# A retention and MLP kernel on one core: a small early read of w1, a last tile in pieces of 384 and 128 columns, and a written-out order of all tasks

## The chip, the cores and the metric

The kernel runs on one core of one Trainium2 chip. The time is device microseconds from one execution of the program; the median of 13 runs of the kernel before is 217.83 us, from 217.11 to 220.94. Engines are named as the profile names them: PE multiplies matrices, DVE and ACT do elementwise work, POOL issues the loads and does a little elementwise work, SP issues stores and transposing transfers.

## The reference

Two stages are chained. The first is a linear attention with a decaying state, over 4 batches, 8 heads, 768 positions and a head width of 64. The second normalises each row of 512, multiplies by a gain, and adds a two-layer MLP with a hidden width of 2048.

```python
gamma = 1.0 - 2.0 ** (-5.0 - np.arange(H))
for t in range(S):
    state = gamma[None, :, None, None] * state + np.einsum('bhd,bhe->bhde', k[:, :, t], v[:, :, t])
    y[:, :, t] = scale * np.einsum('bhd,bhde->bhe', q[:, :, t], state)
# x: y with the heads side by side, (4, 768, 512)
xn = (x - mean(x)) / np.sqrt(var(x) + 1e-06) * g_ln
out = x + np.maximum(xn @ w_ch1, 0.0) @ w_ch2
```

Inputs and output are float32; the kernel multiplies in bfloat16.

## The kernel before

The 3072 rows are cut into 24 tiles of 128 positions. The first position block of each of the four batches comes first (tiles 0 to 3), then the other five blocks of each batch in turn. The recurrence is done block by block: inside a block as a masked product, between blocks through a state per batch.

**A tile's attention.** k and q are transposed so that the head width lies on the partitions. For tiles 0 to 7 PE does it (tasks `e_tk` and `e_tq`, L433 to L446); from tile 8 on SP issues a transposing transfer of k and q together (`e_tr`, L458). DVE scales the transposed q (`e_eq`), PE multiplies (`e_pa`, L472), DVE multiplies by the decay mask (`e_am`), and PE multiplies by v and adds the part from the state (`e_py`, L495). The state comes from POOL scaling v (`e_vg`, L537), PE (`e_pd`, L547) and DVE (`e_pb`). DVE takes mean and variance (`e_bn`) and writes the centred row times the gain (`e_xn`, L514); ACT keeps a copy of x (`e_xc`). The centred rows are transposed by PE and copied by ACT for tiles 0 to 7 (`e_tx`, `e_ex`), and by a transposing transfer on SP from tile 8 on (L593). Because ReLU commutes with a positive factor, the division by the standard deviation is left to the end (`e_sq` on ACT, `e_rs` on DVE).

**The MLP.** Tiles form groups of 1 (eight of them), 2 (four) and 4 (two). A task `e_m1` (L622) is 16 matmuls of 128 columns for a group of one, 8 of 256 for a group of two, or 4 of 512 for a group of four; each needs one quarter of w1, and a ReLU (`e_re`, on ACT or DVE) empties its PSUM tile, of which there are two. The second layer (`e_m2`, L660) is four tasks of four matmuls per tile. Its first task waits for all four quarters of w2. DVE then multiplies by the reciprocal deviation and adds x (`e_add`, L672), and SP stores the tile (`e_st`, L678). The last tile is done in two halves of 256 columns, of which ACT stores the second.

**The loads.** POOL issues all loads of q, k, v, w1 and w2 (L371 and L381), which convert to bfloat16 on the way, except for k and q of tile 0, which SP and ACT load. The constants (two iotas, two memsets of the state) are POOL tasks too. From tile 8 on a one-element copy on POOL, which waits for the load three places earlier, stands before each load of q, k and v (`gate`, L386).

**What sets the order.** Nothing runs as it is written: every piece of work is a task, added to a planner (`Plan.add`) with an engine, a duration, a rank and the tasks that it follows. `Plan.order` (L52) repeatedly takes the task that can start first by its own clock, ties going to the lower rank; pads such as `w_pad`, `tr_pad`, `x_pad` and `slack` lengthen planned waits, and `sq_at` keeps the square roots late. The resulting list is written out, so each engine executes its tasks in that order, and waits in place for whatever a task needs. `Plan.fill` (L113) puts matmuls on zeros before PE tasks whose planned start lies in the first 14 us and leaves a gap.

Of the kernel before, what the change touches and what calls it, by code (L numbers as in the profile page):

```python
# [9 lines left out]
FP32 = mybir.dt.float32  # L10
# [4 lines left out]
PE, ACT, DVE, POOL, SP = range(5)  # L15
# [4 lines left out]
              "k3", "q3", "v3", "w1_2", "k4", "q4", "v4", "k5", "q5", "v5", "w1_3", "w2_0",  # L20
              "k6", "q6", "v6", "k7", "q7", "v7", "w2_1", "w2_2", "w2_3"],
    "bufs": {"qsb": 6, "ksb": 5, "vsb": 9, "qk": 8, "tr": 6, "vg": 3, "trq": 3, "trk": 3},
    "load_pad": 600, "w_pad": 1500, "lead": 32, "lead2": 32, "sq_at": 28000, "late_load": 1250, "step": 8, "pace": 8, "ahead": 3,
    "slack": 600, "tr_pad": 4000, "x_pad": 3000, "vg_pad": 1000, "fill": 0.8, "fill_end": 14000,
}


class Plan:
# [20 lines left out]
        self.tasks.append(t)  # L49
        return t  # L50

    def order(self):  # L52
        left, ends = {}, {}
        for t in self.tasks:
            for u in t["uses"]:
                left[u] = left.get(u, 0) + 1
        held = {name: [] for name in self.bufs}
        engines = sorted(self.seen)
        free = dict(self.begin)
        todo = {e: [t for t in self.tasks if e in t["on"]] for e in engines}  # L60
        sw_free, hw_free, out = self.first_load, 0, []
        while any(todo.values()):
            best = None
            for e in engines:
                for t in todo[e]:
                    if any("end" not in d for d in t["after"] + t["follows"]):
                        continue
                    at = max(free[e], t["at"], sw_free - 7000 if t["load"] else 0)
                    for d in t["after"]:
                        if d["eng"] == e and not d["load"] and not d["hw"]:  # L70
                            at = max(at, d["end"])
                        else:
                            at = max(at, d["seen"] + t["slack"])
                    if t["takes"]:
                        name = t["takes"][0]
                        if len(held[name]) == self.bufs[name]:
                            oldest = held[name][0]
                            if left[oldest]:
                                continue
                            at = max(at, ends[oldest])  # L80
                    if best is None or (at, t["rank"]) < best[0]:
                        best = (at, t["rank"]), t, e
            if best is None:
                raise RuntimeError("no task can start")
            (at, _), t, e = best
            for x in t["on"]:
                todo[x].remove(t)
            t["eng"], t["start"], t["ns"] = e, at, t["on"][e]
            t["end"] = free[e] = at + t["ns"]
            t["seen"] = t["end"] + self.seen[e] + t["lat"]  # L90
            if t["load"]:
                sw_free = max(t["end"] + 800, sw_free) + t["load"]
                t["seen"] = sw_free + 700 + t["lat"]
            if t["hw"]:
                begun = max(at + 600, hw_free)
                queued = max(0, sw_free - begun)
                hw_free = begun + t["hw"] + min(queued, 2 * t["hw"])
                if queued:
                    sw_free += t["hw"] * 2 // 3
                t["end"] = free[e] = max(t["end"], hw_free - 900)  # L100
                t["seen"] = hw_free + 1050 + t["lat"]
            if t["takes"]:
                name = t["takes"][0]
                if len(held[name]) == self.bufs[name]:
                    held[name].pop(0)
                held[name].append(t["takes"])
            for u in t["uses"]:
                left[u] -= 1
                ends[u] = max(ends.get(u, 0), t["seen"])
            out.append(t)  # L110
        return out
# [16 lines left out]
def kernel(  # L128
# [16 lines left out]
    nc = tc.nc  # L145

    B, H, S, D = q.shape
    DM = H * D
    DH = 4 * DM
    P = 128  # L150
    C = S // P
    NT = B * C
    KO = DM // P
# [3 lines left out]
    number = {bc: t for t, bc in enumerate(TILES)}  # L157
# [6 lines left out]
    FILL, FILL_END = CFG["fill"], CFG["fill_end"]  # L164
# [20 lines left out]
    const = ctx.enter_context(tc.tile_pool(name="const", bufs=1))  # L185
# [10 lines left out]
    held = {}  # L196
# [31 lines left out]
    gb = const.tile([P, DM], FP32, name="gb")  # L228
    bns = const.tile([P, NT, 6], FP32, name="bns")
    mv = const.tile([P, NT, 2], FP32, name="mv")  # L230
    rstd = const.tile([P, NT], FP32, name="rstd")
    w1 = const.tile([P, KO, DH], BF16, name="w1")
    w2 = const.tile([P, HO, DM], BF16, name="w2")
# [55 lines left out]
    a = plan.add  # L289
# [109 lines left out]
        load(x, j, pool_rank.get(f"{x}_{j}" if x[0] == "w" else f"{x}{j}", 20 * i))  # L399
    for t, x in ((iota, "iota"), (ipos, "pos")):  # L400
        t["rank"] = pool_rank[x]

    unit, u, behind = {}, 0, []
    for g in range(NG):
# [12 lines left out]
    for t in range(NT):  # L417
        g, i = group_of[t]
# [230 lines left out]

    loaded_w2 = [loaded["w2", i] for i in range(4)]  # L650
    for t, cols in [(t, slice(0, DM)) for t in range(NT - 1)] + [
            (NT - 1, slice(i * DM // 2, (i + 1) * DM // 2)) for i in range(2)]:
        g, i4 = group_of[t]
        hb, h0 = buf_of[g]
        key = ("tp", ("2", t, cols.start))
# [36 lines left out]
                                 rhs=zeros[:, 0:w], start=True, stop=True)  # L692

    with tc.manual_schedule():
        for t in plan.fill(plan.order(), PE, 1100, FILL_END, FILL, warm):
            t["emit"](t["eng"])


# [28 lines left out]
```

## Time and profile before

| | |
|---|---|
| median of 13 runs | 217.83 us (217.11 to 220.94) |
| the profiled execution's own time | 218.1 us |
| its span, first to last instruction | 216.0 us |
| PE busy | 205.3 us (95%) |
| POOL, DVE, ACT busy | 97.2, 118.4, 83.7 us |
| first-layer matmuls (L626) | 93.4 us, 896 of them |
| second-layer matmuls (L664) | 86.9 us |
| matmuls on zeros (L691) | 6.8 us |
| loads through POOL's queue | 13.37 MB, 82% of the time of 16 DMA engines |

The profile is of one execution. A line of it gives the source line (L626), the engine, the operation and the tiles that are written and read. The page cuts the span into 40 slices and gives each engine's busy share in tenths; a busy PE can be matmuls that overlap, so the distance from one start to the next is the better price. The chain of waits follows the work that ended last back to the start. A load's landing is when its data is there, which is later than its issue on the engine.

### The profile page before, as it was taken

To read this page: it belongs to the slowest core of one execution; us is meant where nothing else is said; L and a number is where in the kernel's file an instruction comes from. 1 tells how busy PE (TensorE), PEld (TensorE's weight loads), DVE (VectorE), ACT (ScalarE), POOL (GpSimd) and SP (SyncE) were. 2 spreads that over 40 slices of the span, in tenths; PEclk is the share of its full clock that TensorE was granted. 3 is DMA by queue.
4 is the path that set the end of the run, shared out by engine and by line. 5 is a ranking of instruction groups with operands and counts; after the bars stand their busy time and mean duration, and the time that the engine had idled before them with its cause. 6 is when DMAs were issued, how large, how long until landed. Compare 5 with 4: busy or idle time off the path is not lost.

```text
span 216.0 us, 4747 instructions
## 1 busy us (share of the span) xinstructions
PE 205.3 (95%) x1942; PEld 133.2 (62%) x1962; DVE 118.4 (55%) x230; ACT 83.7 (39%) x157; POOL 97.2 (45%) x151
## 2 busy tenths in 40 slices
PE   7958898999999999999999999999999999999993
PEld 3437798998855458678577667654454444444453
DVE  6847577993157875666786737866553411011121
ACT  5436586665421116345235225305544214442000
POOL 8979569726968666677874746000000000000000
PEclk9999999999999999999999999999999999999999
DMA  9999999999999999999999999921202120010212
GB/s 129 163 180 181 168 191 171 208 108 126 124 168 173 207 154 147 188 159 164 152 148 175 144 164 173 182 72 28 73 0 73 27 97 27 22 49 3 97 49 97
DMA packets 108359, 26.78 MB, mean 124 GB/s; under 512 B 101041, under 2 KB 105393, under 8 KB 108338
## 3 DMA queue, kind: packets, MB, share of 16 engines
q0 software_dynamic: 77024, 13.37, 82.0%
q1 hardware_dynamic: 30114, 12.72, 27.2%
q10 hardware_dynamic: 1200, 0.39, 0.7%
q8 instruction: 15, 0.25, 0.4%
q14 instruction: 6, 0.05, 0.1%
HBM read 27.27 MB, written 6.29 MB: 155 GB/s over the span
## 4 chain that ended last, share of the span: by engine, by line
PE 82%; DMA 8%; POOL 6%; issue 1%; DVE 0%; POOLq 0%
PE tp L664 38%; PE mm L626 34%; DMA w<-in_moe_w_ch_dram 8%; PE pa L477 3%; PE pd L551 2%; PE py L505 2%; PE py L501 2%; POOL qsb L374 1%; POOL vg L539 1%; POOL v L374 1%; POOL ksb L374 1%; POOL vsb L374 1%; POOL w L382 1%; POOL state L287 0%; PE tp L579 0%
## 5 line engine op out<-in xcount | busy, mean ns | idle before, releaser
L626 PE MATMUL mm<-xnt,w 128*128 128x128 bf16 (+2 forms) x896 | 93.4, 257 | 1.0 <-ACT xnt L203 1.0
L664 PE MATMUL tp<-w,h 128*128 128x512 bf16 (+1 forms) x381 | 86.9, 370 | 1.1 <-issue 0.2
L639 ACT ACTIVATE h<-mm 128x512 bf16<-128x512 f32 x91 | 54.4, 598 | 66.4 <-PE mm L626 65.9
L626 PEld LDWEIGHTS <-w 128*128 128x128 bf16 x896 | 66.2, 98 | 21.3 <-issue 1.0
L664 PEld LDWEIGHTS <-h 128*128 128x128 bf16 x400 | 37.7, 98 | 37.5
L673 DVE SCALAR_TENSOR_TENSOR osb<-tp,rstd,x_all 128x512 f32<-128x512 f32 (+1 forms) x25 | 18.2, 729 | 51.3 <-PE tp L664 49.5
L488 DVE TENSOR_TENSOR asb<-pa,mask 128x1024 bf16<-128x1024 f32 x24 | 29.3, 1222 | 12.8 <-PE pa L477 12.8
L520 DVE BATCH_NORM_STATS2 bns<-py 128x6 f32<-128x512 f32 x24 | 16.7, 695 | 19.7 <-PE py L505 19.6
L526 ACT CAST x_all<-py 128x512 bf16<-128x512 f32 x24 | 14.0, 583 | 28.6 <-DVE xn L515 27.5
L539 POOL TENSOR_TENSOR vg<-vsb,vsc 128x512 bf16<-128x512 bf16 x16 | 16.7, 1045 | 8.8 <-DMA vsb<-in_v_dram 6.4
L374 POOL DMA_DIRECT2D vsb<-in_v_dram x20 | 18.2, 911 | 1.7 <-issue 1.7
L515 DVE SCALAR_TENSOR_TENSOR xn<-py,mv,gb 128x512 bf16<-128x512 f32 x24 | 18.0, 751 | 0.9
L565 DVE TENSOR_TENSOR state<-pd,gch 64x256 bf16<-64x256 f32 x40 | 16.7, 418 | 1.6 <-PE pd L551 1.3
L374 POOL DMA_DIRECT2D qk<-in_q_dram x16 | 14.0, 877 | 2.8 <-issue 2.6
L374 POOL DMA_DIRECT2D qk<-in_k_dram x16 | 14.1, 884 | 1.3 <-issue 1.0
L387 POOL COPY scrap<-qk 1x1 bf16<-1x1 bf16 x30 | 5.7, 192 | 13.3 <-DMA qk<-in_k_dram 7.7
L466 DVE TENSOR_TENSOR trq<-tr,qsc 128x512 bf16<-128x512 bf16 x16 | 7.2, 451 | 3.2 <-DMA tr<-qk 3.1
L382 POOL DMA_DIRECT2D w<-in_moe_w_ch_dram x8 | 6.2, 771 | 4.7 <-DMA w<-in_moe_w_ch_dram 4.7
L601 ACT ACTIVATE rstd<-mv,epsb 128x1 f32<-128x1 f32 (+2 forms) x14 | 3.8, 289 | 10.9 <-DVE mv L521 10.9
L691 PE MATMUL pd<-zeros 128*128 128x512 bf16 (+1 forms) x23 | 6.8, 434 | 1.2 <-DVE zeros L237 1.2
L505 PE MATMUL py<-vsb,asb 128*128 128x64 bf16 x160 | 7.9, 193 | 0.0
L501 PEld LDWEIGHTS <-trq 128*128 128x128 bf16 x80 | 6.0, 98 | 3.1
(64 smaller groups left out, 123.2 us busy)
## 6 DMA issues: line engine op xcount, KB each, us to landing
out_dram<-osb SPq DMA_DIRECT2D x23, 256.0 KB, 2.1
w<-in_moe_w_ch_dram POOLq DMA_DIRECT2D x8, 512.0 KB, 9.7
vsb<-in_v_dram POOLq DMA_DIRECT2D x20, 128.0 KB, 5.2
qk<-in_k_dram POOLq DMA_DIRECT2D x16, 128.0 KB, 4.5
qk<-in_q_dram POOLq DMA_DIRECT2D x16, 128.0 KB, 5.0
qsb<-in_q_dram POOLq DMA_DIRECT2D x7, 128.0 KB, 8.5
v<-in_v_dram POOLq DMA_DIRECT2D x4, 128.0 KB, 7.7
ksb<-in_k_dram POOLq DMA_DIRECT2D x4, 128.0 KB, 9.1
```

The lines of the kernel that those rows point to most:

```text
L374: nc.gpsimd.dma_start(out=tile_of(kind, j), in_=src)
L488: nc.vector.tensor_tensor(out=take("asb", t, [P, NPAIR, 2, P], BF16).rearrange("p i a t -> p a i t"), in0=held["pa", t], in1=mask.rearrang ...
L505: nc.tensor.matmul(py[:, h, :], lhsT=held["asb", t][:, h // 2, h % 2, :], rhs=tile_of("v", t)[:, h, :], start=(mi == 0), stop=(mi == n - 1))
L515: nc.vector.scalar_tensor_tensor(out=take("xn", t, [P, DM], BF16), in0=held["py", t].rearrange("p h d -> p (h d)"), scalar=mv[:, t, 0:1], ...
L520: nc.vector.bn_stats(out=bns[:, t, :], in_=held["py", t].rearrange("p h d -> p (h d)"))
L526: nc.scalar.copy(out=x_all[:, t, :].rearrange("p (h d) -> p h d", d=D), in_=held["py", t])
L539: e.tensor_tensor(out=take("vg", j, [P, H, D], BF16), in0=tile_of("v", j), in1=vsc[:, cc, :].unsqueeze(2).to_broadcast([P, H, D]), op=ALU. ...
L565: nc.vector.tensor_tensor(out=held["pb", n][o, :, o], in0=held["pd", b][o, :, o], in1=gch[o, cc, :].unsqueeze(2).to_broadcast([D, NPAIR, D ...
L626: nc.tensor.matmul(p[:, j, :], lhsT=w1[:, ko, (ho + j) * P:(ho + j + 1) * P], rhs=held["xnt", hb][:, h0:h0 + n, ko, :], start=(ko == 0), s ...
L639: nc.scalar.activation(out=dst, in_=src, func=AF.Relu)
L664: nc.tensor.matmul(held[key], lhsT=held["h1", hb][:, ho, i * P:(i + 1) * P], rhs=w2[:, ho, cols], start=(ho == 0), stop=(ho == HO - 1))
L673: nc.vector.scalar_tensor_tensor(out=take("osb", key, [P, w], FP32), in0=held[key], scalar=rstd[:, t:t + 1], in1=x_all[:, t, cols], op0=AL ...
```

## The change

Three things change.

1. A task on SP reads columns 0 to 15 of every row of w1 into a tile `touch` that nothing uses. Its rank is -140.
2. The last tile's output is cut at column 384 instead of 256; SP stores the first piece, ACT the second.
3. `Plan.order` no longer searches. It takes a list `ORDER` of task numbers, in which a number is a task's place among those added (10000 and up also chooses among the engines that may run it), and executes the tasks in that order. The planned times serve only `Plan.fill`. Ranks, `slack` and `sq_at` are no longer read; `w_pad`, `tr_pad` and `x_pad` get smaller.

```diff
-    "load_pad": 600, "w_pad": 1500, "lead": 32, "lead2": 32, "sq_at": 28000, "late_load": 1250, "step": 8, "pace": 8, "ahead": 3,
-    "slack": 600, "tr_pad": 4000, "x_pad": 3000, "vg_pad": 1000, "fill": 0.8, "fill_end": 14000,
+    "load_pad": 600, "w_pad": 550, "lead": 32, "lead2": 32, "sq_at": 28000, "late_load": 1250, "tail": (0, 384, 512), "step": 8, "pace": 8, "ahead": 3,
+    "slack": 600, "tr_pad": 3000, "x_pad": 2000, "vg_pad": 1000, "fill": 0.8, "fill_end": 14000,
 }
+ORDER = [int(x) for x in """
+15 18 14 23 3 8 19 2 27 24 13 26 22 25 44 16 17 45 0 4 7 6 5 28 146 20 21 9 147 10 149 1
...
+314 306 307 690 700 315 298 145 679 327 80 316 311 83 81 540 308 541 538 710 82 84 539
...
+816 817
+""".split()]
...
-    def order(self):
+    def order(self, seq):
...
+        for number in seq:
+            t = self.tasks[number % 10000]
+            e = sorted(t["on"])[number // 10000 % 10]
+            at = max(free[e], sw_free - 7000 if t["load"] else 0)
+            for d in t["after"]:
+                own = d["eng"] == e and not d["load"] and not d["hw"]
+                at = max(at, d["end"] if own else d["seen"])
...
+    touch = const.tile([P, KO, 16], FP32, name="touch")
...
+    a(SP, 390, -140, lambda eng: nc.sync.dma_start(out=touch, in_=w1_v[:, :, 0:16]), hw=400)
...
-            (NT - 1, slice(i * DM // 2, (i + 1) * DM // 2)) for i in range(2)]:
+            (NT - 1, slice(i, j)) for i, j in zip(CFG["tail"], CFG["tail"][1:])]:
...
-        for t in plan.fill(plan.order(), PE, 1100, FILL_END, FILL, warm):
+        for t in plan.fill(plan.order(ORDER), PE, 1100, FILL_END, FILL, warm):
```

Counting the tasks as they are added gives the new order of each engine. POOL's first tasks were iota, iota, v0, k1, q1, v1, the first quarter of w1, k2, q2, the second quarter, v2; they become k1, iota, iota, q2, q1, the memsets of the state, k2, v0, v1, the first and the second quarter of w1, v2. After the fourth quarter of w1 came the first of w2, six tile loads and the other three quarters; now come eight tile loads, one quarter, v8, and the other three, so that k, q and v of tile 8 lie ahead of the last of w2. PE's first tasks were the transposes and product of tile 0, the gain's broadcast and tile 1's transposes; they become nearly the same with k of tile 1 earlier. The first second-layer task was tile 0's, after the first-layer tasks of tiles 0 to 5; it becomes tile 2's, after those of tiles 0 to 5 and two of tile 6. The task numbered 145 is the read into `touch`.

## The prediction

> **What bounds the kernel now.** I read the page first, then busy time by stretch, the chain of waits, and the timeline at both ends.
>
> ```profile
> span 216.0 us, 4747 instructions
> PE 205.3 (95%) x1942; PEld 133.2 (62%) x1962; DVE 118.4 (55%) x230; ACT 83.7 (39%) x157; POOL 97.2 (45%) x151
> DMA  9999999999999999999999999921202120010212
> ```
>
> PE is the bound, and DMA is busy for 26 of the 40 slices. Is PE's 95% all work?
>
> ```profile
> 10.00:15.00 5.00, 2.63 (x38) 1.75 (x36) 2.12 (x3) 1.66 (x3) 3.86 (x7) 1.00 1.69 184
> 20.00:25.00 5.00, 4.03 (x73) 3.49 (x69) 2.86 (x6) 2.93 (x6) 3.04 (x5) 1.00 2.19 164
> 35.00:40.00 5.00, 5.00 (x98) 4.79 (x96) 4.02 (x9) 3.81 (x8) 4.11 (x6) 1.00 1.58 193
> 60.00:80.00 20.00, 19.84 (x156) 10.46 (x158) 14.56 (x25) 2.62 (x5) 14.29 (x24) 1.00 1.70 173
> ```
>
> The first figure after the length is PE's busy time: idle lies before 35 us. The chain gives PE's real prices, by start and length:
>
> ```profile
> 5.14 7.64 DMA w<-in_moe_w_ch_dram
> 21.10 10.02 DMA w<-in_moe_w_ch_dram
> 36.24 0.89 PE mm L626 x16
> 38.47 0.22 PE py L501 x4
> 38.70 0.23 PE py L505 x8
> 39.38 0.33 PE pa L477 x8
> ```
>
> So the first quarter of w1 lands at 12.78 and the fourth at 31.12; a unit of 16 first-layer matmuls takes 0.893 (1.79 for 32), four small matmuls 0.22. By 49.49, where the first second-layer matmul starts, PE has done 24 units (21.4), 24 sets of four transposes (5.3), 8 pa (2.6), 8 py (4 of 0.23, 4 of 0.45: 2.7), 6 pd (1.3) and g's broadcast (1.1): 34.4 us. **15.1 us are lost by then**, to start-up, matmuls on zeros and waits. The whole program has 84.4 (L626) + 83.1 (L664) + 29.7 (rest) = 197.2 us of such work and its last matmul ends at 212.75, 15.5 lost: after 49.5 us only some 0.4 us go. Two places can move: the head, where PE waits for loads, and the tail.
>
> ```profile
> 13.69 0.40 PE L437 MATMUL tp<-idn,k 128*128 128x128 bf16 x4 [2.24 <-DMA k<-in_k_dram]
> 14.15 1.06 PE L626 MATMUL mm<-xnt,w 128*128 128x128 bf16 x16
> 211.06 0.48 DVE L673 SCALAR_TENSOR_TENSOR osb<-tp,rstd,x_all 128x256 f32<-128x256 f32 x1 [1.05 <-PE tp L664]
> 212.75 0.48 DVE L673 SCALAR_TENSOR_TENSOR osb<-tp,rstd,x_all 128x256 f32<-128x256 f32 x1 [1.21 <-PE tp L664]
> 213.26 0.36 ACTq L680 DMA_DIRECT2D out_dram<-osb  x1
> ```
>
> POOL's loads land strictly in their order. The landing records show 0.84 us per tile of k, q or v and 2.55 per weight quarter, without a gap up to 48.9 us, so the order of loads sets when each piece is there. Three weight loads waited on POOL (4.7 us together), each until the load eight places before it had landed.
>
> [...] the load behind the first transpose lands after 2.47 instead of 0.84, so a transpose costs it 1.6. [...]
>
> **Part 1, the small read.** It is the 146th task added, number 145. That number stands far down the fixed list: on SP's queue it follows the transpose of xn for tile 9 and precedes the store of tile 1. In the kernel before these neighbours issue near 66 to 71 us, when all of w1 is long in. It warms nothing. Cost: one issue (0.33 to 0.40 in SP's rows) and 512 pieces of 64 B. Its 32 KB at the tile loads' rate (256 KB read in 0.84) take 0.1; at the 32 ns that the trace's 128 B packets take, over 16 engines, 1.0. It delays loads that PE is not waiting for: 0, up to 1.0 if that cover is gone.
>
> **Part 2, the last tile.** PE: 16 matmuls of 384 and 16 of 128 columns cost 16 x 0.163 + 0.89 = 3.5, as 32 of 256 (0.109 each) do now. The 384 price is between 0.109 for 256 and 0.216 for 512. The add falls from 0.48; 0.75 for 512 and 0.48 for 256 give 0.35 for 128: -0.13. The store of 256 KB lands after 2.0 and that of 128 KB after 1.71, so 64 KB after some 1.57: -0.14. The larger piece ends sooner: its add (0.62) starts 0.89 before PE's end and its store lands some 1.7 after PE's end, the smaller one 1.95. **Tail -0.25** (-0.35 to 0).
>
> **Part 3, the order, head.** POOL's first items are now k1, pos, iota, q2, q1, the two state memsets, k2, v0, v1, then two w1 quarters. By the rows (k1 1.06, iotas 0.43, loads 0.9, memsets 1.01): k1 0.83, q2 2.3, q1 3.2, memsets 4.1, k2 5.1, v0 6.0, v1 7.0, first quarter 7.95 against 5.14. Its landing, X: with its measured 7.64 it is 15.6. The lower end takes the 4.5 of the very first load plus 2.55 - 0.84: 14.15. In the kernel before, one load ahead of it (v1) took 2.49 instead of 0.84; if that comes again the upper end holds. The loads up to the fourth quarter are the same set in both orders, and the 1.4 us of POOL work inside them outweighs the start 0.54 earlier, which also speaks for the upper end. I take X = 15.4.
>
> Tile 0 is not later than that: v0 lands at 10.5; py 0.4, statistics 0.88, xn 0.75, transposes and copy 1.0 give 13.6. The table load may now come after the two casts at 4.8; mask and product then end near 11, still 14.3.
>
> After X: second quarter X+2.55, v2 +3.4, k3 +4.25, q3 +5.1, third +7.65 (8.15 if it is slow by 0.5, as now), fourth +16.1 (16.6). PE walks its list: unit, pa2, tx1 to X+1.45; waits 1.15 for the second quarter; unit, py2 to 3.75; waits 0.55 for k3; then to 7.3; waits 0.35 to 0.85 for the third; then to 12.4 to 12.9. The first square root now stands on ACT ahead of a ReLU that the unit after next needs: its table load holds PE some 0.6. Then 17.1 to 17.6, past the fourth quarter's landing, and 15 units (13.4), 4 pa, 8 transposes' sets, 3 py, 3 pd (5.1): X+35.6 to 36.1, with 0.3 for small gaps X+36.15 in the middle, 51.55. By then 26 units, 9 pa and the rest are done: 36.6. **Lost 15.0 against 15.1: the head moves by -0.1**; -1.4 with X = 14.15, +0.35 with both upper ends.
>
> Warm-up matmuls on zeros go from five groups to seven; they fill waits for loads and cost nothing unless PE is awaited, up to 0.5.
>
> The last w2 piece now has three tile loads more ahead of it (2.5): nine tiles and four quarters after the fourth w1 quarter, X+34 to 34.5, plus 1.6 for tile 8's transpose, now issued during these loads: 51.0 to 51.5 against PE's 51.55. Hidden, barely.
>
> **The middle.** Pads and slack only move planned times. PE lost about 0.4 here; the new list puts stores ahead of transposes on SP (13's store ahead of tile 21's transpose, with some 10 us of PE work between their uses against add 0.75, issue 1.3, landing 5.1, product 0.49). I take +0.3 (0 to +1.5).
>
> **Sum:** -0.25 - 0.1 + 0.3 = -0.05: span 215.95, with the 2.1 around it 218.05 against this execution's 218.1. The median is 0.27 lower: 217.8.
>
> **Rivals.** *Early weights*: v1's 2.49 was a start-up accident that doesn't recur. For it: loads before v1 take 0.84 to 0.93. Against it: it coincides with w1's first reads. Head -1.4, sum -1.35: 216.5. *Late w2*, the slower side: the first second-layer matmul stands in PE's order and waits for all w2. Every microsecond of the last quarter past 51.55 costs one; from 52.0 on it decides. One further transpose (1.6) or an issue held on POOL by the copies that wait for k8 and q8 suffices: +0.5 to +2, 219.0. For it: the margin is below 0.6; against it: POOL's last weight issue falls near 40. *A new stall in the middle*, a transpose behind a store: +1.2, 219.0. The small read doing its work early is excluded by its place.
>
> **How the numbers follow.** About 0.2% (0.44 us) is what can be told from no change. Main case 0.45, its own range 217.1 to 218.6, half of it within 0.44, 0.10 below, 0.13 above; early weights 0.20; late w2 0.20 and a stall in the middle 0.15. So faster 0.30, same 0.22, slower 0.48. The range reaches from early weights with the whole tail gain (216.1) to late w2 with some of the middle's loss (219.7).
>
> **What would show it.** The first quarter issued near 8 us and landed near 15.4; first L664 matmul near 51.5 with no wait for a weight load; the small read on SP near 70 us; last add 0.35. It is wrong if the first unit starts before 14.5, if that matmul waits for w2, or if PE is idle for over 1 us after 60 us.

## The result, and the profile after

The changed kernel is slower: a median of 228.57 us in 11 runs (223.79 to 229.89), against 217.85 us in 48 runs of the kernel before. The ratio is 1.0349, with a 95% interval of 1.0309 to 1.0389. The forecast was 217.8 us, within 216.1 to 219.7. The ratios leave out every run over 1.5% above the fastest of the same kernel, which is six of these eleven, so that a ratio of 1.0349 (7.6 us) and a difference of medians of 10.7 us stand side by side. Sums below are made with ratios; where an experiment has none, its median is given alone. The profiled execution took 226.96 us.

The page after, with the span, the engines' busy time, and three rows of tenths in 40 slices:

```profile
span 225.2 us, 4740 instructions
PE 208.7 (93%) x1948; PEld 134.7 (60%) x1970; DVE 118.5 (53%) x230; ACT 82.2 (36%) x157; POOL 97.4 (43%) x151
PE   3798999989999989937999999999999999999994
PEclk9999999999999999995999999999999999999999
DMA  9999999999799999999999999778931212002032
```

The rows of PE and its clock in the kernel before:

```profile
PE   7958898999999999999999999999999999999993
PEclk9999999999999999999999999999999999999999
```

After the head the changed kernel's PE has its 8s and 9s except in slices 18 and 19, with 3 and 7 tenths; in slice 19 the granted clock is down to 5 tenths. DMA is busy for 29 slices (before: 26). Busy time by stretch (PE's first after the length, then PEld, DVE, ACT, POOL, granted clock, DMA share, GB/s):

```profile
10.00:15.00 5.00, 4.95 (x50) 3.02 (x50) 3.19 (x5) 1.75 (x3) 4.65 (x6) 1.00 1.34 182
60.00:80.00 20.00, 19.84 (x176) 11.57 (x176) 10.06 (x20) 3.94 (x7) 9.98 (x18) 1.00 1.41 142
100.00:107.00 7.00, 4.51 (x18) 2.56 (x19) 0.00 (x0) 0.60 (x1) 5.30 (x9) 0.53 1.55 159
```

The stretches that the prediction looked at are no worse than before (from 20 to 25 and from 35 to 40 us, not shown here, PE is busy for all of the 5.00 us); 4.95 of 5.00 between 10 and 15 us is PE busy with little work (x50) and with zeros. The loss is in two other places. What PE waited for in the whole execution (us in total, times, longest; its wait for the first zeros, 1.2 us as before, is left out):

```profile
PE mm L657 <- DMA xnt<-xn: 5.4, 2, 4.7
PE tp L468 <- ACT k L231: 3.5, 1, 3.5
PE pa L508 <- DVE trq L497: 0.9, 1, 0.9
```

One wait of 4.66 us, ending at 102.49, is for the transposed xn of tiles 10 and 11, the input of their first-layer unit; one of 3.46 us stands at the head, before tile 0's first transpose. The first matmul of the second layer (L664 in the kernel before, and so called below; L695 here) starts at 53.26, and the last ends at 222.17. With the prediction's prices for the work done by then taken off (36.6 and 197.2 us), 16.7 us are lost at the head and 25.0 in all: the head is worse by 1.6 and the rest by 7.9 than in the execution before (15.1 and 15.5).

**The head.** ACT in the first microseconds, of the kernel before and then of the changed one (start, length, line, operation):

```profile
1.87 1.28 ACT L266 ACT_TABLE_LOAD   x1 [1.87 <-issue]
3.92 0.60 ACT L203 CAST k<-osb 128x512 bf16<-128x512 f32 x1
```

```profile
0.73 0.48 ACTq L374 DMA_DIRECT2D osb<-in_q_dram  x1
4.89 1.28 ACT L231 ACT_TABLE_LOAD   x1 [4.89 <-DMA osb<-in_k_dram]
6.18 0.62 ACT L231 CAST k<-osb 128x512 bf16<-128x512 f32 x1
```

In both executions the table load, 1.28 us, stands in front of ACT's first activation. That was one without an input from outside; now it is the cast of k, so the load starts only at 4.89, behind the landing of k; ACT's half of k lands at 4.82 instead of 3.81, issued at 1.24 behind the half of q instead of at 0.73. PE then (same columns):

```profile
1.19 2.21 PE L722 MATMUL pd<-zeros 128*128 128x512 bf16 x7 [1.19 <-DVE zeros L266]
6.86 0.61 PE L468 MATMUL tp<-idn,k 128*128 128x128 bf16 x4 [3.46 <-ACT k L231]
7.26 1.38 PE L722 MATMUL pd<-zeros 128*128 128x512 bf16 x5
8.43 0.63 PE L475 MATMUL tp<-idn,qsb 128*128 128x128 bf16 x4
8.86 1.59 PE L722 MATMUL pd<-zeros 128*128 128x512 bf16 x4
```

After 3.46 us of idleness the first record of a full clock is at 11.61 us (before: 5.15); until then four transposes take 0.6 us instead of 0.4, and the groups of zeros between them, 1.38 and 1.59 us, stand in tile 0's chain. The first unit starts at 17.38 instead of 14.15.

**Tile 8.** The chain of waits between 30 and 60 us:

```profile
31.49 5.10 DMA qk<-in_q_dram
36.59 0.02 issue
36.60 13.58 DMA tr<-qk
50.18 0.02 issue
50.20 0.44 DVE trq L497
```

Tile 8's transposes are issued at 36.60, beside the second-layer weights, and take 13.58 us; the next two take 4.44 and 4.80 (58.31 to 62.75, 64.11 to 68.91). Each slows the other: the landing steps of the four pieces of w2 are 4.28, 3.41, 2.98 and 2.61 us instead of 2.55, and v8, among them, has 4.17. In the kernel before, tile 8's transposes are issued at 48.12, when the last of w2 has landed (46.36), and take 5.11; the steps of w2 are 2.49 to 2.58. Where a run below puts tile 8 behind w2, the steps are 2.55 to 2.96 and its transposes take 2.82.

**The loads of tiles 9 on.** POOL's timeline (idle before and what ended it in brackets). L416 is a gate, a one-element copy that waits for an earlier load (gates stand before the loads of tiles 9 to 23, in both kernels); L403 issues a load:

```profile
68.76 0.18 POOL L416 COPY scrap<-vsb 1x1 bf16<-1x1 bf16 x1 [1.04 <-DMA vsb<-in_v_dram]
71.68 0.18 POOL L416 COPY scrap<-qk 1x1 bf16<-1x1 bf16 x1 [2.74 <-DMA qk<-in_q_dram]
72.14 0.87 POOL L403 DMA_DIRECT2D vsb<-in_v_dram  x1 [0.28 <-DMA qk<-in_k_dram]
...
73.99 0.88 POOL L403 DMA_DIRECT2D qk<-in_k_dram  x1
76.83 0.36 POOL L416 COPY scrap<-vsb 1x1 bf16<-1x1 bf16 x1 [1.96 <-DMA vsb<-in_v_dram]
80.85 0.18 POOL L416 COPY scrap<-qk 1x1 bf16<-1x1 bf16 x1 [3.65 <-DMA qk<-in_q_dram]
81.31 0.88 POOL L403 DMA_DIRECT2D qk<-in_q_dram  x1 [0.28 <-issue]
82.17 0.88 POOL L403 DMA_DIRECT2D vsb<-in_v_dram  x1
```

Each load of the kernel before stands directly behind its own gate. In this list, from tile 12 on, two gates stand in a row eight times, with their loads behind them. A load whose own gate is open waits at the other gate as well: v of tile 13, whose gate opens at 76.83, is issued at 82.17. Between 74.9 and 81.3 us POOL issues nothing; the three loads issued last land at 76.71, 80.73 and 81.43. What POOL waited for at its gates, before and after:

```profile
POOL scrap L387 <- DMA qk<-in_k_dram: 7.7, 4, 4.6
POOL scrap L387 <- DMA qk<-in_q_dram: 5.2, 6, 1.5
POOL scrap L387 <- DMA vsb<-in_v_dram: 4.3, 5, 1.3
```

```profile
POOL scrap L416 <- DMA vsb<-in_v_dram: 19.8, 12, 5.6
POOL scrap L416 <- DMA qk<-in_q_dram: 12.4, 8, 3.7
POOL scrap L416 <- DMA qk<-in_k_dram: 8.9, 4, 6.7
```

That is 17.2 us before and 41.1 after. q of tile 14 lands at 91.99 instead of 81.89. Of these 10.1 us, 5.2 are there at k of tile 9 (56.59 against 51.37, behind the late w2), and 4.9 are lost from there on, in part because q is the third of a tile's loads here and the second before. SP works its list in order: tile 14's transposes, waiting for that q, stand at 92.14 in front of the transposes of xn for tiles 10 and 11, issued at 94.04 and 95.41 and landing at 102.35. PE waits until 102.49, and its clock is half from 100.36 to 107.19.

### The profile page after: what moved, and what is told of

It is laid out like the page before. It is cut to its first block, busy times and chain, and to the rows that moved or that the text cites. A ratio compares the mean times of both kernels' runs of the same rounds, so it can differ in the third digit from the quotient of the medians.

```text
span 225.2 us, 4740 instructions
## 1 busy us (share of the span) xinstructions
PE 208.7 (93%) x1948; PEld 134.7 (60%) x1970; DVE 118.5 (53%) x230; ACT 82.2 (36%) x157; POOL 97.4 (43%) x151
## 3 DMA queue, kind: packets, MB, share of 16 engines
q0 software_dynamic: 77024, 13.37, 81.3%
## 4 chain that ended last, share of the span: by engine, by line
PE 67%; DMA 19%; POOL 8%; DVE 2%; issue 2%; SPq 0%; POOLq 0%
PE tp L695 33%; PE mm L657 28%; DMA tr<-qk 6%; DMA xnt<-xn 6%; DMA w<-in_moe_w_ch_dram 5%; DMA qk<-in_q_dram 2%; PE pa L508 2%; PE py L536 2%; POOL qsb L403 2%; PE py L532 1%; PE pd L582 1%; POOL k L403 1%; POOL v L403 1%; POOL w L411 1%; POOL vg L570 1%
## 5 line engine op out<-in xcount | busy, mean ns | idle before, releaser
L657 PE MATMUL mm<-xnt,w 128*128 128x128 bf16 (+2 forms) x896 | 97.5, 259 | 5.8 <-DMA xnt<-xn 5.4
L695 PE MATMUL tp<-w,h 128*128 128x512 bf16 (+2 forms) x379 | 90.2, 373 | 1.5 <-issue 0.6
L695 PEld LDWEIGHTS <-h 128*128 128x128 bf16 x400 | 37.2, 98 | 36.7 <-issue 0.6
L704 DVE SCALAR_TENSOR_TENSOR osb<-tp,rstd,x_all 128x512 f32<-128x512 f32 (+2 forms) x25 | 18.2, 726 | 28.4 <-PE tp L695 28.2
L551 DVE BATCH_NORM_STATS2 bns<-py 128x6 f32<-128x512 f32 x24 | 16.7, 695 | 17.1 <-PE py L536 16.9
L596 DVE TENSOR_TENSOR state<-pd,gch 64x256 bf16<-64x256 f32 x40 | 16.7, 418 | 13.5 <-PE pd L582 13.2
L570 POOL TENSOR_TENSOR vg<-vsb,vsc 128x512 bf16<-128x512 bf16 x16 | 16.7, 1045 | 10.5 <-PE pd L582 9.2
L403 POOL DMA_DIRECT2D vsb<-in_v_dram x20 | 18.0, 901 | 2.8 <-issue 2.0
L403 POOL DMA_DIRECT2D qk<-in_k_dram x16 | 14.4, 902 | 1.9 <-issue 1.3
L403 POOL DMA_DIRECT2D qk<-in_q_dram x16 | 14.2, 887 | 2.0 <-issue 2.0
L416 POOL COPY scrap<-qk 1x1 bf16<-1x1 bf16 x30 | 5.3, 177 | 21.4 <-DMA qk<-in_q_dram 12.4
L638 DVE RECIPROCAL rstd<-rstd 128x1 f32<-128x1 f32 (+2 forms) x14 | 2.0, 155 | 18.8 <-ACT rstd L632 18.7
L416 POOL COPY scrap<-vsb 1x1 bf16<-1x1 bf16 x15 | 3.0, 202 | 19.8 <-DMA vsb<-in_v_dram 19.8
L722 PE MATMUL pd<-zeros 128*128 128x512 bf16 (+1 forms) x31 | 8.4, 412 | 1.2 <-DVE zeros L266 1.2
L536 PEld LDWEIGHTS <-asb 128*128 128x128 bf16 x192 | 7.8, 98 | 0.3
```

Source lines behind the costliest of these rows:

```text
L403: nc.gpsimd.dma_start(out=tile_of(kind, j), in_=src)
L536: nc.tensor.matmul(py[:, h, :], lhsT=held["asb", t][:, h // 2, h % 2, :], rhs=tile_of("v", t)[:, h, :], start=(mi == 0), stop=(mi == n - 1))
L551: nc.vector.bn_stats(out=bns[:, t, :], in_=held["py", t].rearrange("p h d -> p (h d)"))
L570: e.tensor_tensor(out=take("vg", j, [P, H, D], BF16), in0=tile_of("v", j), in1=vsc[:, cc, :].unsqueeze(2).to_broadcast([P, H, D]), op=ALU. ...
L596: nc.vector.tensor_tensor(out=held["pb", n][o, :, o], in0=held["pd", b][o, :, o], in1=gch[o, cc, :].unsqueeze(2).to_broadcast([D, NPAIR, D ...
L657: nc.tensor.matmul(p[:, j, :], lhsT=w1[:, ko, (ho + j) * P:(ho + j + 1) * P], rhs=held["xnt", hb][:, h0:h0 + n, ko, :], start=(ko == 0), s ...
```

## The experiments

In the first theory the head and SP's order carry the loss; the theory of the gates came last, and three runs test it.

**The tail alone, in the kernel before.**

```diff
-            (NT - 1, slice(i * DM // 2, (i + 1) * DM // 2)) for i in range(2)]:
+            (NT - 1, slice(i, j)) for i, j in ((0, 384), (384, 512))]:
```

> The kernel before with only the last tile's pieces changed to 384 and 128 columns. Theory of the prediction: the tail gets 0.25 us shorter (last add 0.35 instead of 0.48, its store landing 0.14 sooner), so about 217.6 against 217.85, a ratio near 0.999. Rival: the two stores at the end share the 16 DMA engines and the smaller one lands no sooner; then only the add's 0.13 is seen or nothing, ratio 1.000.

Measured: 217.80 against 217.96 us, ratio 0.9995 (0.9966 to 1.0024). The piece's own lines are as worked out (below), but a gain of 0.25 us cannot be told from none.

**The small read, left out and early.** In the first run, the changed kernel without it; in the second, it is issued fourth on SP, together with the early table load described next.

```diff
-    a(SP, 390, -140, lambda eng: nc.sync.dma_start(out=touch, in_=w1_v[:, :, 0:16]), hw=400)
+    a(SP, 390, -140, lambda eng: None, hw=400)
```

> The changed kernel without the small read of w1 (its task issues nothing; nothing read it, so the output is the same). Theory: it stands at 76 us on SP, its 512 pieces share the DMA engines with tile 9's transpose of xn, on which PE waits 0.7 us: the time falls by 0 to 1 us. Rival: it delays the loads behind it and so feeds the stall at 98 us: the time falls by 2 us or more.

> As the run with ACT's first tasks altered, and the small read of w1 is issued fourth on SP, near 2.2 us, where its rank would put it. Theory that w1's first reads are slow and a read ahead cures it: v0 and v1 ahead of the first quarter land 0.84 apart (2.0 and 1.2 in the changed kernel), the first quarter lands 1 us or more sooner than 14.8, and the 0.6 us that PE waited for the second quarter go. Rival: the delay has to do with the DMA engines getting out of step, not with w1: the first quarter lands at 14.8 or later, since 512 more small pieces are ahead of it.

Left out: a median of 226.65 us (221.38 to 229.36), with a wait of 5.38 us on the transposed xn at 102.87, so it plays no part in it. Early: 223.55 us in two runs, but the first quarter of w1 lands at 15.90 against 15.76 with the same head and a late read. The read does not bring the weights sooner. Why the time is lower than with the early table load alone (226.68) is not shown; in that execution tile 8's transposes hold PE for 2.72 us, until 52.44, and it does not wait near 100 us.

**SP's order.** The transposes of xn of tiles 10 and 11 ahead of tile 14's transposes.

```diff
+ORDER = moved(ORDER, [312, 324], 350)
```

> The changed kernel with two tasks moved on SP: the transposes of xn for tiles 10 and 11 stand ahead of tile 14's transpose instead of behind it. Theory A (order on SP): they issue at some 86 to 88 us instead of 94 and 95.4, land by 92, PE doesn't wait the 4.7 us before the first unit of tiles 10 and 11 and its clock isn't halved afterwards (some 3 us more): span about 218 to 219. Theory B (the loads are late by 10 us and PE would be short of work anyway): the wait turns up at the next transposes or products, and the span falls by less than 3 us.

Measured: 223.34 us, ratio 1.0230 (1.0176 to 1.0283). The wait of 4.66 us is gone and the clock stays full, but waits of 1.20, 1.66 and 1.03 us on other transposed xn appear at 81.7, 116.0 and 155.2 us. So this place is real and worth about one per cent (1.0349 to 1.0230), and the new waits point to something upstream that is late for all of them. The next run goes further, with SP's whole order as in the kernel before, in the changed kernel:

> The changed kernel with all of SP's tasks in the order that they had before (the small read kept behind tile 9's transpose of xn); the other engines keep the new order. Theory A: the transposes of xn no longer stand behind transposes of later tiles, the waits at 81 and 98 us and the small ones that moving two tasks left (1.2, 1.7, 1.0) go: 220 to 221, the rest being the head. Theory C: late loads leave these waits in place, 223 as with two tasks moved.

It took 241.26 us, ratio 1.1118, with a wait of 8.23 us for transposed xn at 169.88. The order of one engine cannot be put back without those that feed it.

**The head alone, and tile 8 alone.** First: a one-element activation early on ACT, so that the table is loaded while ACT waits, and the half of k issued ahead of q's.

```diff
+ORDER = moved(ORDER, [0], 15)
+ORDER = moved(ORDER, [8], 17)
+ORDER = moved(ORDER, [16], 19)
...
-    table = a(ACT, 1300, -100, lambda eng: None, at=1800)
+    hot = const.tile([1, 1], FP32, name="hot")
+    table = a(ACT, 1300, -100, lambda eng: nc.scalar.activation(
+        out=hot, in_=zeros[0:1, 0:1], func=AF.Exp, bias=0.0, scale=1.0), at=1800)
```

> The changed kernel with ACT's first tasks altered: a one-element Exp on a zeroed tile ahead of the cast of k, so that the table load runs while k is still on its way, and ACT's half of k issued ahead of its half of q. Theory: the cast of k ends at 4.5 instead of 6.8, tile 0's chain and the first unit of the first layer come 2 us sooner (15.4 instead of 17.4, then bound by w1's first quarter at 14.8), and the first second-layer matmul some 1 to 2 us sooner than 53.3; the late stall near 98 us stays. Rival: the start is hidden, since loads bound the first 50 us: the first second-layer matmul stays at 53 and the time is the same within 0.5.

The head moved as thought: tile 0's first transpose at 4.66, clock full from 9.11, the first unit at 15.81. But the time is 226.68 us, ratio 1.0391 (1.0331 to 1.0451): PE comes sooner and waits longer, 2.07 us for tile 8's transposes and 2.65 us at 101.74, and the first L664 is at 54.33, not before 53.26. Then tile 8's loads behind w2:

```diff
+ORDER = moved(ORDER, [52, 53, 54, 55, 57, 59], 56)
+ORDER = moved(ORDER, [275], 284)
+ORDER = moved(ORDER, [276, 277, 278], 528)
+ORDER = moved(ORDER, [279, 280, 281], 675)
```

> The changed kernel with tile 8 put back: its loads of k, q and v stand behind the last quarter of w2 instead of ahead of three of them, and its transpose, product and output follow later on SP, DVE and PE. Theory C (tile 8's transpose beside the w2 loads is what made the loads late: it took 13.6 us, and the last w2 quarter landed at 55.8 instead of 49 to 50): the last w2 quarter lands near 48 to 50, the loads of the tiles after it come some 5 us sooner, the first transposes of xn are in time, and the stalls at 81 and 98 us shrink to under 1 us each: time 219 to 221. Theory A (SP's order alone): the w2 loads come sooner but tile 14's transpose still holds those of tiles 10 and 11, and most of the 4.7 us stall stays: 224 or more.

The last of w2 lands at 49.96 instead of 55.75 and PE no longer waits for tile 8, but k of tile 9 lands at 56.67, as in the changed kernel, and 2.80 us are waited at 102.03: 226.42 us, ratio 1.0392. This edit leaves three gates in a row ahead of k of tile 9: its own opens at 50.86, the load is issued at 53.09. So tile 8's part is not tested cleanly here. Head, tile 8 and SP's whole old order together:

> The changed kernel with SP's order of before, tile 8 put back behind w2, and ACT's first tasks altered (early table load, k ahead of q). If these three places hold the loss: first unit at 15.8, first second-layer matmul near 50.5 to 51.5, no wait of PE over 0.7 us after that, time 217.5 to 219, level with the kernel before. If the rest of the new order is worse by itself (POOL's list, PE's list): 220 or more.

242.68 us, ratio 1.1046: SP's order outweighs the rest.

So mending what comes earlier brings nothing while the loads of tiles 9 on arrive when they do.

**The order of a tile's three loads.** In the changed kernel q is loaded last; these runs load k, q, v, alone, and with head and SP's moved transposes.

```diff
-load k, load v, load q     (POOL, tiles 9 to 19)
+load k, load q, load v
```

This is the edit in words; in the kernel it is a permutation of numbers in `ORDER`.

> The changed kernel, but the loads of tiles 9 to 19 are issued in the order k, q, v instead of k, v, q (the order of all other work as changed). Theory D (the middle is lost because each tile's q is its last load, so that SP's transposes wait for a load at almost every tile, and everything behind them on SP waits too): the idle time of PE at 102 us, 4.66 us on the transposed xn of tiles 10 and 11, falls below 3 us, the half clock behind it shortens or goes, and the median is 2 to 4 us under the changed kernel's 228.6, at about 225. Rival (the loads themselves are late by about 10 us, and which of a tile's three comes last does not matter): the idle time stays within 1 us of 4.66 and the median within 1 us of the changed kernel.

> The changed kernel with three parts undone together: q before v in the loads of tiles 9 to 19, the transposes of xn of tiles 10 and 11 ahead of tile 14's transpose on SP, and at the head the table load first on ACT with k's half issued ahead of q's. If the loss is the late head plus SP's order plus the order of the loads, as the theory of this study says: first unit at 15.8, no idle time of PE over 2 us after 60 us, clock full from 9.1 on except behind tile 8's transpose at 52 us, and a median of 219 to 222. If the order of the work is bound as a whole (undoing one wait only opens the next): a median of 223 or more, with new waits on xn of 1 to 3 us each.

The first took 221.85 us (217.86 to 222.48, four runs), a larger gain than was hoped: q of tile 14 lands at 89.00 and there is no wait at 102 us. The combination took 223.20, ratio 1.0209 (1.0153 to 1.0266), not the sum of its parts. The next three tell whether this order is the cause: k, v, q alone in the kernel before, and the head, then head and tile 8, added to it in the changed one.

> The kernel before, but the loads of tiles 9 to 22 are issued in the order k, v, q instead of k, q, v; the order of everything else, and of each engine's other work, stays as before. Theory D (the order of a tile's three loads sets when its transposes can start): q lands one load, 1.2 to 1.5 us, later per tile, idle times of PE of 0.5 to 2 us appear between 60 and 130 us, and the median is 1 to 5 us above 217.5 (ratio 1.005 to 1.023). Rival (the order of before has more slack on its transposes than one load, so it alone costs nothing): ratio 0.998 to 1.002.

> The changed kernel with q before v in the loads of tiles 9 to 19, and at the head the table load first on ACT with k's half issued ahead of q's; the order of SP as changed. Measured so far: q before v alone 221.85, both of these and the moved transposes of xn together 223.2. If the moved transposes are what held the combination back: 219.5 to 221.5. If the head gives nothing at the end because tile 8's transpose then waits longer (PE idle over 2 us at 51 us): 221.5 to 224, with the first L664 no sooner than 54.

> The same, and tile 8's loads put behind those of w2 (as in the kernel before), with its transposes after them. If what is left of the loss is tile 8's transpose beside w2: no idle time of PE over 1 us near 51 us, first L664 at 51 to 52.5, no idle time over 2 us later, last product at 214 to 216 and a median of 218.5 to 220.5, within 3 us of the kernel before. If the loads of tiles 9 on, late by the same time, take it back: idle times on the transposed xn of over 2 us near 80 to 102 us and a median over 222.

In the kernel before that order costs nothing: ratio 1.0001 (0.9982 to 1.0020). In the changed kernel the head gives 222.75 us (1.0217), and head and tile 8 give 223.84 us (1.0269), where a wait of 4.16 us, ending at 99.49, is back:

```profile
PE mm L660 <- DMA xnt<-xn: 4.2, 1, 4.2
```

So the order of the three loads is not the cause by itself, although alone it brought the median down as far as the unpaired gates will below (221.89). Loading q before v had brought tile 14's q forward by 3 us. With head and tile 8 mended as well it lands no sooner (88.91), but PE runs out of work at 95.33 instead of 97.83, and waits again. What makes all loads late remained, and POOL's timeline above shows the pairs of gates.

**The clock.** 42 matmuls on zeros ahead of the waiting unit, written into its own accumulator, which the unit then overwrites:

```diff
                 p = take("mm", key, [P, two, n * P], FP32)
+                for _ in range(42 if (g, ho) == (9, 0) else 0):
+                    nc.tensor.matmul(p[:, 0, :], lhsT=zeros[:, 0:P],
+                                     rhs=zeros[:, 0:n * P], start=True, stop=True)
```

> The changed kernel with 42 matmuls of zeros (128x256) issued by PE just ahead of the unit that waits 4.66 us at 102 us; they write into the unit's own accumulator and are overwritten by its first real product. Nothing else is changed, and the stall itself is not shortened. Theory: the 6.8 us at half clock from 100.4 to 107.2 are a cost of the idle time, apart from the wait itself: with PE kept busy through the wait the clock stays full there, the eight products of 128x256 that took 1.86 us take 1.04 again, and the profile's end comes 2.5 to 3.5 us sooner (median about 225.5). Rival: the half clock has another cause (power, the load of DMA), or the wait is followed by others that take the 3 us back: the clock still drops near 100 us, or the median stays within 1 us of the changed kernel.

The window from 100 to 107 us in this run, to be set against the 0.53 above:

```profile
100.00:107.00 7.00, 6.95 (x64) 5.91 (x63) 0.58 (x1) 0.60 (x1) 5.80 (x11) 1.00 1.50 164
```

The clock stays full, so here it was the idle time that halved it. The zeros hold the unit from 99.63 to 104.21, 4.58 us and so nearly as long as the wait of 4.66, and from the first unit of tiles 8 and 9 to the last matmul PE needs 138.1 us instead of 140.7. The total is not better, though: 226.79 us, ratio 1.0372 (1.0313 to 1.0430). PE came there 2 us later in this execution, in which tile 8's transposes had held it for 2.93 us and the clock was halved at 51.57 (mean 0.66 from 51 to 56 us); the transposed xn had landed at 101.20, so the zeros kept the unit 3.0 us longer than its input did. The local price of 2.5 us is shown; that filling the wait shortens the program is not.

**The pairs of gates.** Every load stands directly behind its own gate again; the loads' order stays k, v, q. With that, k of tile 9 comes ahead of the last quarter of w2.

```diff
-gate k, load k, gate v, gate q, load v, load q     (POOL, tiles 9 to 23)
+gate k, load k, gate v, load v, gate q, load q
```

Again the edit in words, for the most frequent pattern.

> The changed kernel, with only POOL's gates and loads of tiles 9 to 23 in another order: each load stands directly behind its own gate (gate k, load k, gate v, load v, gate q, load q), as in the kernel before, where the changed order has two gates in a row and then two loads. The order of a tile's loads stays k, v, q; nothing else moves. Theory E (the loads are late because a load waits at another tile's gate too, with one transfer or none in flight): POOL's longest waits at the gates fall from 5.6 and 6.7 us to under 3, q of tile 14 lands at 84 to 88 us instead of 91.99, the idle time at 102 us falls under 2 us, the clock stays full, and the median is 220 to 224 (3 to 8 us less than 228.6, of which the head keeps 1.6 and tile 8 some 2). Rival (the loads are late by the head and the volume of DMA alone, a gate more or less does not matter): q of tile 14 within 1.5 us of 91.99, median over 226.

221.89 us, ratio 1.0163 (1.0122 to 1.0204). q of tile 14 lands at 88.55, less early than expected. The waits at the gates are 28.3 us in total, though the longest is still 5.4, where under 3 was expected:

```profile
POOL scrap L417 <- DMA vsb<-in_v_dram: 11.6, 8, 5.4
POOL scrap L417 <- DMA qk<-in_q_dram: 9.7, 8, 2.0
POOL scrap L417 <- DMA qk<-in_k_dram: 7.0, 5, 4.6
```

No wait on transposed xn is left in PE's list, whose largest are now

```profile
PE tp L469 <- ACT k L232: 3.4, 1, 3.4
PE pa L509 <- DVE trq L498: 1.9, 1, 1.9
```

These are the head and tile 8. The next run takes them out too, and loads q before v up to tile 19:

> The same, with k, q, v as the order of the loads of tiles 9 to 19, tile 8's loads behind those of w2, and the early table load and k ahead of q on ACT. With paired gates this combination took 223.84 and stood idle 4.16 us at 99.49 us. Theory E: first L664 at 51 to 52, no idle time of PE over 1.5 us after it, median 217.5 to 220. Rival: the idle time at 99 us stays over 3 us, and the median over 222.

219.64 us, ratio 1.0087 (1.0048 to 1.0127), the first unit at 15.16, the first L664 at 50.77, the mean clock of the profiled execution 1.000. The same combination with paired gates had taken 223.84 (1.0269), so unpairing gives 1.8 points here and 1.9 alone. PE's list:

```profile
PE pa L511 <- DVE trq L500: 2.2, 2, 1.5
PE tp L471 <- ACT k L232: 1.5, 1, 1.5
```

Last, pairs of gates in the kernel before:

```diff
+        for t in range(9, NT):
+            i, j = out.index(loaded["q", t]), out.index(gates["v", t - 1])
+            out[i], out[j] = out[j], out[i]
```

> The kernel before with POOL's gates in pairs, and nothing else changed: for tiles 9 to 23 the gate of v stands ahead of the load of q (gate k, load k, gate q, gate v, load q, load v). Theory E in the kernel it did not come from: fewer loads in flight, the loads slower by 0.3 to 0.5 us each, q of tile 14 lands 4 to 10 us later than 81.89, and the median is 1 to 8 us above 217.5. If the kernel before has its loads so far ahead that later ones cost nothing (as k, v, q cost nothing there): ratio 0.998 to 1.003 although q of tile 14 is later; then the pairs hurt only where the loads already start late.

222.95 us against 218.27, ratio 1.0184 (1.0122 to 1.0247). q of tile 14 lands at 86.52, and POOL's waits at its gates are

```profile
POOL scrap L387 <- DMA vsb<-in_v_dram: 20.3, 15, 3.1
POOL scrap L387 <- DMA qk<-in_q_dram: 16.1, 13, 2.8
POOL scrap L387 <- DMA qk<-in_k_dram: 4.7, 2, 4.5
```

which is 41.1 us, by chance the sum of the changed kernel. The exchange makes 15 pairs, one at every tile, where the changed kernel has eight, and at ten tiles it leaves POOL's scaling of v (about 1.05 us) between a pair and its loads, which the kernel before has nowhere. What PE misses first is the scaled v, which POOL computes behind its gates and loads, with no wait for v itself in the longest case:

```profile
PE pd L552 <- POOL vg L540: 4.1, 3, 2.6
```

A wait of 2.6 us ends at 145.52 and the clock is half from 145.84 to 149.25 (mean 0.97 from 110 to 160 us). So pairs cost time in this order too, 1.8 points, though PE feels them at another place. That the size is that of the changed kernel shows little: there are more pairs here, and the part of the scaling is not separated.

**Anything better than both?** In the kernel before, the tail in 384 and 128, and tile 1's py and tile 0's first unit moved ahead of the transpose of tile 2's k, where PE stood idle 2.24 us.

```diff
+        for x in (m1s[0, 0], pys[1]):
+            out.remove(x)
+            out.insert(out.index(tks[2]), x)
+        out.remove(pys[1])
+        out.insert(out.index(m1s[0, 0]), pys[1])
```

> The kernel before with the output of the last tile in pieces of 384 and 128 columns, and on PE tile 1's py and the first unit of the first layer, m1 of tile 0, moved ahead of the transpose of tile 2's k. In the kernel before PE stands idle 2.24 us at 13.69 us while the first quarter of w1 has landed. If the idle time at the head is on the path: first L664 0.5 to 1 us sooner than 49.49, median 217.0 to 217.5 against 217.8, ratio 0.996 to 0.999. If the loads of tiles 3 to 8 and of w2 set the time of the first second-layer product instead: the same work waits later, ratio 0.999 to 1.001. If tile 2 is late because of it: up to 1 us slower.

217.99 us, ratio 1.0011 (0.9990 to 1.0033). PE then waits 1.6 us for the first quarter of w1, and the clock is half from 15.2 to 22.0 us (the execution's mean is 0.983). No version here beats the kernel before.

## Why the prediction was wrong

Taken as points of ratio, and undone in this sequence, the loss of 3.5 is made of 1.9 for the pairs of gates (1.0349 to 1.0163), 0.8 for the head, tile 8 and the order of three loads together (to 1.0087), and 0.9 that is left; each ratio is known to about 0.4. Another sequence would share it out differently, since the loads' order alone had brought the median to 221.85. The cause of the rest is open. What is in sight there was not tried: the first L664 is 1.3 us later than in the kernel before, and two waits of 0.68 and 1.55 us for transposes end at 93.66 and 132.77.

**The middle, the step that failed.** "I take +0.3 (0 to +1.5)" had looked at SP's stores ahead of its transposes. Those were no trouble. POOL's list behind tile 8 was not followed, although the prediction knew that the gates stand there and that the order of loads sets when each piece lands. The term, put at 0.3 us, is 1.9 points, some 4 us, for the pairs alone; in the profiled executions 226.96 becomes 221.66. The sign named for being wrong, PE idle over 1 us after 60 us, is what the profile shows. The rival "a new stall in the middle" had the place, a transpose on SP behind something else, but it named a store where it was a load, and +1.2 us where it was 4.66 and the half clock.

**The head.** The first quarter of w1 was well worked out: issued at 7.97 (7.95), landed at 14.77 (15.4, within 14.15 to 15.6). It fell at "Tile 0 is not later than that". The table load was seen as 0.7 us after the casts; it stands between the landing of k and its cast, with PE idle 3.46 us, and the clock was not in the sum at all. Zeros that "cost nothing unless PE is awaited, up to 0.5" stood in tile 0's chain, before the clock was full. The first unit started at 17.38 and the head lost 1.6 us more, not 0.1 less. The clock was full at 11.61 us instead of 5.15, and four transposes ahead of it take 0.61 to 0.63 us, behind it 0.39 to 0.40. Such a term belonged into every step that moved PE's first work.

**The last of w2.** 51.0 to 51.5 was expected, 55.75 came. One transposing transfer was priced at 1.6 us of the loads' time, and that price was misread: the load with the step of 2.47 was issued only at 47.48 and landed 3.89 us later, and no load that POOL issues in that trace lands within 3.46 us of its issue, so at most 0.4 of the step can be the transpose's. Beside w2 it was far dearer: four pieces of w2 and v8 took 6.4 more than their rates (17.45 us between the landings of 38.31 and 55.75, against 4 x 2.55 + 0.84). It went in both directions: the transposes took 13.58 us for their part, against 5.11 in the kernel before and 2.82 in the run that puts tile 8 behind w2. The rival "late w2" expected the first L664 to wait for all of w2. It started at 53.26, 2.5 us before the last quarter landed; the plan lists all four, but this matmul did not wait for the one that was still missing.

**Right.** The small read: it warms nothing, where it stands or early, and what it costs cannot be told in these few runs. It sat even later than thought:

```profile
L432 SPq DMA_DIRECT2D touch<-in_moe_w_ch_dram x1: 687/687/687, 76.2 to 76.2; - x1
```

And the tail, whose adds are as worked out (0.62 and 0.35); from the last matmul to the last landing it takes 2.04 us instead of 2.26:

```profile
221.31 0.62 DVE L704 SCALAR_TENSOR_TENSOR osb<-tp,rstd,x_all 128x384 f32<-128x384 f32 x1 [1.85 <-PE tp L695]
222.21 0.35 DVE L704 SCALAR_TENSOR_TENSOR osb<-tp,rstd,x_all 128x128 f32<-128x128 f32 x1 [0.27 <-PE tp L695]
```

## What to carry to other kernels

When a change rewrites the order of all engines, follow the queue that issues the loads to its end, and look at each instruction on it that waits: two waits in a row ahead of two loads let the slower hold both. Taking such pairs out gave 1.8 and 1.9 points in two versions of the changed order, and putting them into the old order, with POOL's scaling of v shifted as well, cost 1.8. Where half clock follows a wait of PE, as 6.83 us of it followed the 4.66 us here, it belongs to the wait's price. And mending what lies before a late transfer gains nothing until that transfer is early: head and tile 8 gave nothing, alone or together, while the gates were paired; with the gates unpaired these two and the loads' order gave 0.8 together.

## What was not expected of the hardware

- The half clock came late and stayed past the wait. In the changed kernel PE stands idle from 97.83 to 102.49 us, and the granted clock is half from 100.36 to 107.19, 6.83 us: it falls 2.53 us into the wait and is full again 4.70 us after PE's work has come back. Eight matmuls of 128x256 take 1.86 us at 102.49 and 1.04 at 109.79.
- The length of a wait does not decide alone. Behind the wait of 2.6 us in the kernel before with pairs of gates the clock was half for 3.41 us; the profiled execution with tile 8 behind w2, with a wait of 2.80 us, has a mean clock of 1.000. The one without the small read, with a wait of 5.38 us, has 0.992, and that of the changed kernel, with 4.66 us, 0.985. These executions differ in other things too, and the filled wait is the only experiment on it; what else decides was not shown.
- The eleven runs of the changed kernel have mean clocks of 0.992, 0.985 and 0.978; the profiled one, with its 6.83 us at half, has 0.985. They took 223.79 to 227.10, 226.19 to 229.76, and 229.88 to 229.89 us.
- From the start the first record of a full clock is at 5.15 us in the kernel before and at 11.61 in the changed one. Tile 0's four transposes of k take 0.61 us ahead of it in both, at 4.58 and at 6.86; four transposes behind it take 0.40, at 7.58 and at 12.51.
- The transposes of tile 8's k and q took 13.58 us in the changed kernel, beside the loads of w2. The longest of any other tile took 5.01 us in that execution, and 6.04 in the kernel before.
